# Three more score tiles on VectorE, a bank of its own for the first tile, and set-up work moved to GpSimd, in a softcap attention followed by a soft mixture of experts

## The chip, the cores and the metric

The kernel runs on one core of one Trainium2 chip. The metric is device time in microseconds (us). The engines in the profile are PE (TensorE's products, with PEld for its weight loads), DVE (VectorE), ACT (ScalarE), POOL (GpSimd) and SP (SyncE). Each engine works through its own instructions in the order written and waits at an instruction until what it needs from others is there.

## The reference

Attention over 8 batches, 12 heads, 448 positions and head dimension 64, with a soft cap of 30 on the scores, and then a soft mixture of 8 experts with 4 slots each:

```
scores = q @ k.T / 8;  scores = 30 * tanh(scores / 30)
attn = softmax(scores);  x = attn @ v            # laid out as 3584 x 768
logits = x @ phi                                  # 3584 x 32
slot_input = softmax(logits over tokens).T @ x    # 32 x 768
slot_out[e] = relu(slot_input[e] @ w1[e]) @ w2[e] # 768 -> 1024 -> 768
out = softmax(logits over slots) @ slot_out
```

Since the cap bounds the scores, the kernel takes exp without subtracting a maximum. The inputs are float32; the kernel works in bfloat16.

## The kernel before, in words

**Tiles.** Four heads form a quad; there are 24 quads, and each has two pairs of heads (`h` = 0 and 1), 48 pairs in all. A score tile is 128 key rows (64 of each of the pair's two heads) by 448 queries; a pair has seven of them. The 336 tiles go in the order `order` through 56 chunks of six tiles, and each chunk through two halves of three tiles. A half takes a score buffer of three banks of PSUM (`psS`, two buffers). One more bank (`psV`) is shared by the products with v, some transposes and filler products, and one (`psT`) by the other transposes.

**Stages of a chunk** (lines 831 to 861). ScalarE takes tanh of a half from PSUM into a buffer of SBUF (L326; five such buffers, one a chunk), and then exp in place for the tiles of a chunk that are its own (L330). Chunks 0 and 1 have their exp in their own round, later chunks one round later. PE makes the scores (L317) two halves ahead, and three rounds or so later the products of exp with v (`pv`, L581), whose right side is a block matrix `vbd` with v on its diagonal blocks, zeros elsewhere and a column of ones for the sums. VectorE divides by the sums (L588, L591). GpSimd casts v into the block matrix (L287), issues the loads of q and k (L184, as bfloat16) and of the experts' weights (L116, L120). SyncE's queue issues the loads of v (L194).

**Tiles on VectorE.** `SHARED` gives for some chunks the number of tiles, counted from the chunk's first, whose exp VectorE computes in place of ScalarE: a cubic in eight steps (`poly_exp`, L555 to L563), on one, two or three tiles at once. `POLY` writes out by hand at which place of which round each step stands; `(9, '>a'): ((9, 0), ...)` puts step 0 of chunk 9 behind what else stands at place `a` of round 9. The places of a round are, in order, 0, m, e (after the two tanh), a (after the first products with v), b (after the first half's scores), r, c, d (after the second half's scores); `<` and `>` put an item before or behind the others of its place.

**The order around it.** `at(j, place, function)` puts transposes, casts, loads and fillers at such places; `quad_in` does so for the casts, transposes and v casts of a quad. `transp` (L277, for the second quad L274) turns q and k on PE and copies the result out on VectorE (L279). A filler (`spare`, `busy`, `fill`: L814, L817, L611) is a product whose result nobody reads. `spare` takes a tile of `psV`.

**The start.** Quad 0 and quad 1 are loaded as float32 (`load_first`). Quad 0 is cast and turned in pieces by ScalarE, VectorE and PE (`first_half`, `first_pieces`, L231, L235, L237). Quad 1 is cast by VectorE (`cast`, L265), its v by GpSimd (L287, after which, for quad 0, SyncE loads the next v). The two block matrices are set by VectorE (`init_vbd`, L302 to L304) at place c of rounds 0 and 1. The first tanh is split: one tile, then two.

**After the attention** (from L862) come the last pairs, the slots' sums, the two layers of the experts and the output products.

Of the kernel before, what the change touches and what calls it, by code (L numbers as in the profile page):

```python
# [9 lines left out]
F32 = mybir.dt.float32  # L10
# [20 lines left out]
VW = 2 * W  # L31
# [6 lines left out]
def kernel(  # L38
# [20 lines left out]
    cap = float(cap)  # L59
    qk_scale = 1.0 / (DH ** 0.5)  # L60
# [178 lines left out]
    def first_half(h):  # L239
        for nm in ("k", "q"):  # L240
            if h == 0:
                qkT[nm, 0] = qk[0].tile([P, NT, P], BF16, name=nm + "T", tag=nm + "T")
        one = psT.tile([P, 8, P], BF16, name="ps1", tag="T")
        two = psV.tile([P, NT, P], BF16, name="ps2", tag="pv")
        if h == 0:

            three = boots[1][:, CS - 1, :].bitcast(BF16).rearrange("p (c q) -> p c q", q=P)
            first_pieces(h, (("cast", "q", 4, NT, act, None, 0), ("cast", "k", 0, CS, dve, None, 0),
                             ("cast", "q", 0, 4, dve, None, 0), ("turn", "q", 4, NT, pe, three, 0),
                             ("turn", "k", 0, CS, pe, two, 0), ("copy", "q", 4, NT, act, three, 0),  # L250
                             ("turn", "q", 0, 4, pe, one, 0), ("copy", "k", 0, CS, dve, two, 0),
                             ("cast", "k", CS, NT, act, None, 0), ("copy", "q", 0, 4, dve, one, 0),
                             ("junk", "k", 2, 0, pe, None, 0), ("turn", "k", CS, NT, pe, three, 3),
                             ("junk", "k", 1, 0, pe, None, 0), ("copy", "k", CS, NT, dve, three, 3)))
        else:
            first_pieces(h, (("cast", "k", 0, NT, dve, None, 0), ("cast", "q", 0, NT, dve, None, 0),
                             ("turn", "k", 0, NT, pe, two, 0), ("turn", "q", 0, NT, pe, one, 0),
                             ("copy", "k", 0, NT, dve, two, 0), ("copy", "q", 0, NT, dve, one, 0)))
            for nm in ("q", "k"):
                raws.pop((nm, 0)), casts.pop((nm, 0))  # L260
                load(nm, 2)

    def cast(nm):

        dve.tensor_copy(casts[nm, 1].rearrange("p c (h d) -> p h c d", h=2),  # L265
                        raws.pop((nm, 1)).rearrange("p h (c d) -> p h c d", d=DH))
# [32 lines left out]

    def init_vbd(n):  # L300
        t = vbds[n]
        dve.memset(t, 0.0)  # L302
        dve.memset(t[0:HP, :, :, DH:DH + 1], 1.0)
        dve.memset(t[HP:P, :, :, VW - 1:VW], 1.0)  # L304

    scores, exs, pvs, xq, xTs, lps = {}, {}, {}, {}, {}, {}

    def qk_chunk(i):
        sc = psS.tile([P, CS, 512], F32, name="sc", tag="sc")
        scores[i] = sc  # L310
        for u in range(CS):
            pr, c = order[i * CS + u]
            Q, h = divmod(pr, 2)
            r = slice(h * HP, h * HP + HP)
            for n in range(2):
                cs = slice(n * HP, n * HP + HP)
                pe.matmul(sc[cs, u, 0:S], qkT["k", Q][r, c, cs],  # L317
                          qkT["q", Q][r, :, cs], start=True, stop=True)

    def tanh_chunk(i):  # L320
        j, half = divmod(i, CH // CS)
        if half == 0:
            exs[j] = exps[j % NEX].tile([P, CH, S], BF16, name="ex", tag="ex")
        sc = scores.pop(i)
        for u0, u1 in ((0, 1), (1, CS)) if i == 0 else ((0, CS),):
            act.activation(exs[j][:, half * CS + u0:half * CS + u1, :].bitcast(F16),  # L326
                           sc[:, u0:u1, 0:S], ACT.Tanh, scale=qk_scale / cap)

    def exp_part(j, u0, u1):
        act.activation(exs[j][:, u0:u1, :], exs[j][:, u0:u1, :].bitcast(F16), ACT.Exp, scale=cap)  # L330
# [1 line left out]
    def exp_chunk(j):  # L332
# [1 line left out]

    SHARED = {3: (1, 0), 4: (3, 0), 6: (1, 0), 7: (3, 0), 9: (3, 0), 11: (2, 0), 12: (3, 0), 14: (3, 0),
# [4 lines left out]
    POLY = {(3, '>b'): ((3, 0), (3, 1)),  # L342
            (3, 'r'): ((3, 2),),
            (3, '<c'): ((3, 3),),
            (3, '>d'): ((3, 4),),
            (4, '>a'): ((3, 5), (3, 6), (4, 0)),
            (4, '>b'): ((3, 7),),
            (4, '<c'): ((4, 1),),
            (5, 'e'): ((4, 2), (4, 3)),
            (5, '>b'): ((4, 4),),  # L350
            (5, 'r'): ((4, 5),),
            (5, '>c'): ((4, 6),),
            (6, 'e'): ((6, 0), (6, 1)),
            (6, '>b'): ((6, 2), (6, 3)),
            (6, 'r'): ((4, 7),),
            (6, '>c'): ((6, 4), (6, 5)),
            (7, 'e'): ((7, 0), (6, 6), (6, 7)),
            (7, '>b'): ((7, 1),),
            (7, '>c'): ((7, 2), (7, 3)),
            (7, '>d'): ((7, 4),),  # L360
            (8, '>b'): ((7, 5),),
            (8, '>c'): ((7, 6),),
            (8, '>d'): ((7, 7),),
            (9, '>a'): ((9, 0),),
            (9, '>b'): ((9, 1),),
            (9, '>c'): ((9, 2),),
            (9, '>d'): ((9, 3),),
            (10, 'e'): ((9, 4),),
            (10, '>a'): ((9, 5),),
            (10, '>d'): ((9, 6),),  # L370
            (11, 'e'): ((11, 0), (9, 7)),
            (11, '>a'): ((11, 1), (11, 2)),
# [291 lines left out]
    es = {}  # L664
# [65 lines left out]
    def at(j, slot, f, *a):  # L730
        if j < 0:
            j, slot = 0, "b"
        aux.setdefault((j, slot), []).append((f, a))
# [16 lines left out]
                for n in range(2):  # L750
                    at(*v_in, vcast, Q, n)

    WHEN = {'k1': (-1, 'd'), 'q1': (0, 'b'), 'v1': (3, 'c'), 'k2': (2, 'b'), 'q2': (2, 'd'), 'v2': (7, 'b'), 'k3': (4, 'b'), 'q3': (5, 'b'), 'v3': (11, 'c'), 'x0': (5, 'a'), 'x1': (8, 'd'), 'x2': (10, 'a'), 'lg': (10, 'd'), 'ee': (11, 'm'), 'ss': (11, 'c'), 'et': (13, 'a'), 'en': (14, 'c'), 'es': (15, 'a')}

    for b in range(B):
        j, p = b * PER, 6 * b

        def when(nm):
            return j + WHEN[nm][0], WHEN[nm][1]

        if b == 0:
            quad_in(1, (0, "a"), (0, "b"), (0, "d"), (1, "a"), (2, "d"))
        else:
            quad_in(3 * b + 1, (j - 1, "b"), (j, "a"), when("k1"), when("q1"), when("v1"))
        quad_in(3 * b + 2, (j, "d"), (j + 1, "c"), when("k2"), when("q2"), when("v2"))
        quad_in(3 * b + 3, (j + 4, "a"), (j + 5, "a"), when("k3"), when("q3"), when("v3"))
        if b == 0:
            at(j + 1, "d", spare, 34)
            at(j + 2, "d", spare, 4)
        for k, slot, f, n in FILL:  # L770
            if (b or k > 2) and j + k < NCH - 1:
                at(j + k, slot, f, n)
        for hq in range(NQB if b < B - 1 else 1):
            at(*when(f"x{hq}"), x_transp, NQB * b + hq)
        if b == B - 1:
            at(j + 6, "a", x_transp, NQ - 2, (0,))
        if b < B - 1:
# [9 lines left out]
            at(j, slot, poly_exp, chunk, shared[chunk][0], n)  # L787
    for n, job in enumerate(wjobs):
        at(1 + n * (NCH - 5) // len(wjobs), "b", *job)
    for j, slot, n in ((0, "a", 10), (0, "c", 10), (1, "b", 10), (1, "c", 8)):  # L790
        at(j, slot, spare, n, 1)
    LATE = ((52, 'd', 3, 1), (54, 'd', 3, 3),)
    for j, slot, n, parts in LATE:
        at(j, slot, spare, n, parts)
    at(0, "c", init_vbd, 0)
    at(1, "c", init_vbd, 1)
    for n in range(2):
        at(0, "d", vcast, 0, n)
# [373 lines left out]
```

## Time and profile before

| what | value |
|---|---|
| time, median of three runs | 291.37 us (289.97 to 292.13) |
| time of the profiled execution | 290.2 us |
| its span | 288.4 us |
| busy: PE, DVE, ACT, POOL | 252.4, 239.7, 255.4, 134.6 us |
| first tanh starts | 7.00 us |
| mean granted clock of PE | 0.983 |

The span is what the profile covers of the execution's time; 1.8 us lie outside it. Busy times count each engine's own instructions, for PE with the fillers. The profile's views used below are the totals, the slices of the span, busy time per stretch, the instructions in order of time, and groups of instructions. In a row in order of time the first number is the start and the second the length; neighbours of the same kind may be merged into one row with a count, and a bracket at the end gives the idle time before it and what ended it.

### The profile page before, as it was taken

What the parts mean: (1) busy time and instruction counts of PE and PEld (TensorE: products, weight loads), DVE (VectorE), ACT (ScalarE), POOL (GpSimd) and SP (SyncE); (2) the same over time, 40 slices, a digit from 0 to 9 for tenths busy, and PEclk for the clock granted to TensorE, in tenths of its full rate; (3) what the DMA queues carried; (4) which work ended last, traced back from release to release, by engine and by line L of the source; (5) the groups of instructions that cost most, each with busy time, mean ns of one, the idle gap of its engine ahead of it and who ended that gap; (6) DMA issues with size and microseconds to landing.
All of it is one profiled execution on the core that took longest, in us unless ns stands there. A gap on an engine that the chain in (4) does not pass through costs nothing.

```text
span 288.4 us, 10848 instructions
## 1 busy us (share of the span) xinstructions
PE 252.4 (88%) x4753; PEld 171.2 (59%) x4753; DVE 239.7 (83%) x502; ACT 255.4 (89%) x211; POOL 134.6 (47%) x189
## 2 busy tenths in 40 slices
PE   8898789998999899989898999899899999998810
PEld 7555466656675667566656675666565767642400
DVE  3727899999999999999999999999999986347740
ACT  3999999999999999999999999999999997237720
POOL 4492655564755566555656646574563120200000
PEclk9999999999999999999999999999999999999985
DMA  7999999999999999999999999999999577989995
GB/s 215 263 190 204 195 204 228 226 198 199 232 229 197 200 231 222 224 199 230 226 217 201 223 226 207 215 221 220 212 174 224 114 246 250 406 316 384 414 424 240
DMA packets 58479, 68.11 MB, mean 236 GB/s; under 512 B 4161, under 2 KB 54593, under 8 KB 58433
## 3 DMA queue, kind: packets, MB, share of 16 engines
q0 software_dynamic: 42448, 35.31, 78.5%
q1 hardware_dynamic: 15696, 31.89, 32.0%
q8 instruction: 37, 0.61, 0.8%
q10 hardware_dynamic: 288, 0.23, 0.2%
q14 instruction: 10, 0.07, 0.1%
HBM read 91.72 MB, written 19.27 MB: 385 GB/s over the span
## 4 chain that ended last, share of the span: by engine, by line
DVE 30%; PE 27%; ACT 26%; issue 6%; DMA 3%; POOL 3%; DVEq 0%; ACTq 0%
ACT ex L326 15%; ACT ex L330 10%; PE pv L581 7%; DVE xq L591 5%; PE sc L317 4%; DVE xT L643 3%; DVE xp L561 3%; DVE ex L562 2%; DVE xp L559 2%; PE so_ps L1034 2%; DMA out_dram<-ob 2%; DVE qT L279 2%; PE hp L1006 2%; DVE ex L555 2%; DVE ex L563 2%
## 5 line engine op out<-in xcount | busy, mean ns | idle before, releaser
L326 ACT ACTIVATE ex<-sc 128x1344 f16<-128x1344 f32 (+1 forms) x113 | 150.1, 1459 | 2.0 <-PE sc L317 2.0
L330 ACT ACTIVATE ex<-ex 128x2688 bf16<-128x2688 f16 (+5 forms) x58 | 118.0, 2042 | 0.1
L581 PE MATMUL pv<-vbd,ex 128*128 128x130 bf16 (+1 forms) x1610 | 94.9, 211 | 11.1 <-POOL vbd L287 8.4
L581 PEld LDWEIGHTS <-ex 128*128 128x128 bf16 (+1 forms) x1680 | 75.8, 101 | 36.0 <-PE sc L317 9.0
L287 POOL CAST vbd<-vraw 64x896 bf16<-64x896 f32 x46 | 46.0, 1000 | 53.1 <-issue 23.2
L317 PE MATMUL sc<-qT,kT 64*64 64x448 bf16 x672 | 70.3, 359 | 0.6 <-ACT ex L326 0.4
L591 DVE TENSOR_TENSOR xq<-pv,rec 128x448 bf16<-128x448 f32 x46 | 28.7, 624 | 1.5
L317 PEld LDWEIGHTS <-kT 64*64 64x64 bf16 x672 | 23.8, 105 | 6.3 <-issue 4.3
L295 POOL MEMSET vbd<- 64x1 bf16 x22 | 4.0, 180 | 46.3 <-PE pv L581 46.3
L116 POOL DMA_DIRECT2D w1b<-in_moe_w_dram x32 | 25.0, 783 | 0.0
L559 DVE TENSOR_TENSOR xp<-xp,xf 128x1344 f16<-128x1344 f16 (+2 forms) x33 | 24.0, 726 | 0.6
L562 DVE TENSOR_TENSOR ex<-ex,xp 128x1344 uint16<-128x1344 uint16 (+2 forms) x33 | 24.0, 726 | 0.3
L561 DVE TENSOR_TENSOR xp<-xp,xf 128x1344 f16<-128x1344 f16 (+2 forms) x33 | 23.6, 716 | 0.7
L279 DVE COPY kT<-kps 128x896 bf16<-128x896 bf16 x23 | 14.2, 619 | 4.9 <-PE kps L277 4.6
L184 POOL DMA_DIRECT2D qb<-in_q_dram x22 | 16.6, 755 | 3.3 <-DMA kraw<-in_k_dram 3.3
L611 PE MATMUL pv<-ones 128*128 128x57 bf16 x390 | 16.4, 188 | 0.0
L563 DVE TENSOR_SCALAR ex<-ex 128x1344 uint16<-128x1344 uint16 (+2 forms) x33 | 16.2, 491 | 0.1
L184 POOL DMA_DIRECT2D kb<-in_k_dram x22 | 16.1, 734 | 0.2 <-issue 0.2
L277 PEld LDWEIGHTS <-qb 128*64 128x64 bf16 x308 | 10.1, 109 | 10.2 <-issue 10.2
L558 DVE TENSOR_SCALAR xp<-xf 128x1344 f16<-128x1344 uint16 (+2 forms) x33 | 15.8, 480 | 0.3
L555 DVE TENSOR_SCALAR ex<-ex 128x1344 uint16<-128x1344 f16 (+2 forms) x33 | 15.5, 470 | 0.7 <-ACT ex L326 0.6
L120 POOL DMA_DIRECT2D w2d<-in_moe_w_dram x21 | 15.8, 777 | 0.1
(126 smaller groups left out, 341.3 us busy)
## 6 DMA issues: line engine op xcount, KB each, us to landing
w1b<-in_moe_w_dram POOLq DMA_DIRECT2D x32, 384.0 KB, 8.7
vraw<-in_v_dram SPq DMA_DIRECT2D x44, 224.0 KB, 6.2
w2d<-in_moe_w_dram POOLq DMA_DIRECT2D x21, 384.0 KB, 8.6
w2t<-w2d SPq DMA_DIRECT2D x21, 384.0 KB, 7.4
out_dram<-ob SPq DMA_DIRECT2D x7, 768.0 KB, 7.8
qb<-in_q_dram POOLq DMA_DIRECT2D x22, 224.0 KB, 7.6
kb<-in_k_dram POOLq DMA_DIRECT2D x22, 224.0 KB, 6.5
w2b<-in_moe_w_dram POOLq DMA_DIRECT2D x11, 384.0 KB, 8.5
```

The costliest lines, as they stand in the source:

```text
L116: pool.dma_start(out=w1b[e][:, js, fs], in_=w1r[:, e, js, fs])
L184: pool.dma_start(out=t, in_=quad_ap(nm, Q))
L287: pool.tensor_copy(vbds[Q % 2][r, :, :, c0:c0 + DH], raw[r])
L317: pe.matmul(sc[cs, u, 0:S], qkT["k", Q][r, c, cs], qkT["q", Q][r, :, cs], start=True, stop=True)
L326: act.activation(exs[j][:, half * CS + u0:half * CS + u1, :].bitcast(F16), sc[:, u0:u1, 0:S], ACT.Tanh, scale=qk_scale / cap)
L330: act.activation(exs[j][:, u0:u1, :], exs[j][:, u0:u1, :].bitcast(F16), ACT.Exp, scale=cap)
L559: lambda: dve.tensor_tensor(p, p, f, op=ALU.mult),
L561: lambda: dve.tensor_tensor(p, p, f, op=ALU.mult),
L562: lambda: dve.tensor_tensor(y, y, p, op=ALU.add),
L563: lambda: dve.tensor_scalar(y, y, 128.0 / STEP, 128.0 * (127 - base), ALU.mult, ALU.add))
L581: pe.matmul(out_, exs[j][r, u, q0:q0 + (HP if tail else P)], v_, start=(c == 0 and g == gs[0] < NF), stop=(c == NT - 1), skip_group_check= ...
L591: dve.tensor_tensor(xq[Q][:, h, s0:s1, :], pv[:, 0:s1 - s0, 0:DH], rec.to_broadcast([P, s1 - s0, DH]), op=ALU.mult)
```

## The change

Five parts:

- `SHARED` gives VectorE two tiles of chunk 1 (none before) and two of chunk 3 (one before), 82 tiles in all instead of 79. `POLY` is written anew for chunks 1 to 12; from round 14 on it is the same.
- The first score tile of all is written to a tile of `psV`, a bank of its own, and the first tanh reads it there.
- The casts of the second quad's k and q go from VectorE to GpSimd, both now at place c of round 0, ahead of the first quad's v casts, which stand at the same place instead of d. Its transposes stand together at place d of round 0.
- Both block matrices are set by GpSimd, before the first products, the zeros through a float32 view.
- The counts of the fillers in rounds 0 to 2 are others, and one filler product ahead of the first scores is gone.

The entry `en` that leaves `WHEN` was not read.

```diff
-                             ("junk", "k", 1, 0, pe, None, 0), ("copy", "k", CS, NT, dve, three, 3)))
+                             ("copy", "k", CS, NT, dve, three, 3)))
...
-        dve.tensor_copy(casts[nm, 1].rearrange("p c (h d) -> p h c d", h=2),
-                        raws.pop((nm, 1)).rearrange("p h (c d) -> p h c d", d=DH))
+        pool.tensor_copy(casts[nm, 1].rearrange("p c (h d) -> p h c d", h=2),
+                         raws.pop((nm, 1)).rearrange("p h (c d) -> p h c d", d=DH))
...
-        dve.memset(t, 0.0)
-        dve.memset(t[0:HP, :, :, DH:DH + 1], 1.0)
-        dve.memset(t[HP:P, :, :, VW - 1:VW], 1.0)
+        pool.memset(t.rearrange("p h c w -> p (h c w)").bitcast(F32), 0.0)
+        pool.memset(t[0:HP, :, :, DH:DH + 1], 1.0)
+        pool.memset(t[HP:P, :, :, VW - 1:VW], 1.0)
...
+    own = {}
...
-        sc = psS.tile([P, CS, 512], F32, name="sc", tag="sc")
-        scores[i] = sc
+        scores[i] = psS.tile([P, CS, 512], F32, name="sc", tag="sc")
         for u in range(CS):
+            if i == u == 0:
+                own[0] = psV.tile([P, 1, 512], F32, name="sc0", tag="pv")
+            sc = own[0] if i == u == 0 else scores[i]
...
-                           sc[:, u0:u1, 0:S], ACT.Tanh, scale=qk_scale / cap)
+                           (own[0] if i == u0 == 0 else sc)[:, u0:u1, 0:S], ACT.Tanh,
+                           scale=qk_scale / cap)
...
-    SHARED = {3: (1, 0), 4: (3, 0), 6: (1, 0), ...
+    SHARED = {1: (2, 0), 3: (2, 0), 4: (3, 0), 6: (1, 0), ...
-    POLY = {(3, '>b'): ((3, 0), (3, 1)),
-            (3, 'r'): ((3, 2),),
-            (3, '<c'): ((3, 3),),
-            (3, '>d'): ((3, 4),),
-            (4, '>a'): ((3, 5), (3, 6), (4, 0)),
-            (4, '>b'): ((3, 7),),
...
+    POLY = {(1, 'e'): ((1, 0),),
+            (1, '>b'): ((1, 1), (1, 2)),
+            (1, 'r'): ((1, 3),),
+            (1, '<c'): ((1, 4),),
+            (1, '>c'): ((1, 5),),
+            (2, '>a'): ((1, 6),),
+            (2, '>c'): ((1, 7),),
+            (3, 'e'): ((3, 0), (3, 1), (3, 2)),
+            (3, '>b'): ((3, 3),),
+            (4, '>a'): ((3, 4), (3, 5), (3, 6), (4, 0)),
             (4, '<c'): ((4, 1),),
+            (5, 'e'): ((3, 7), (4, 2)),
+            (5, '>a'): ((4, 3),),
...
-            quad_in(1, (0, "a"), (0, "b"), (0, "d"), (1, "a"), (2, "d"))
+            quad_in(1, (0, "c"), (0, "c"), (0, "d"), (0, "d"), (2, "d"))
...
-            at(j + 1, "d", spare, 34)
-            at(j + 2, "d", spare, 4)
+            at(j + 1, "d", spare, 14)
+            at(j + 2, "d", spare, 5)
...
-    for j, slot, n in ((0, "a", 10), (0, "c", 10), (1, "b", 10), (1, "c", 8)):
+    for j, slot, n in ((0, "a", 5), (0, "c", 16), (1, "b", 12), (1, "c", 3)):
...
-    at(0, "c", init_vbd, 0)
-    at(1, "c", init_vbd, 1)
     for n in range(2):
-        at(0, "d", vcast, 0, n)
+        at(0, "c", vcast, 0, n)
...
     load_first()
+    for n in range(2):
+        init_vbd(n)
```

More of the change, by code (lines that the diff above doesn't have):

```diff
@@ L333, in exp_chunk @@
         exp_part(j, taken(j), CH)
-    SHARED = {3: (1, 0), 4: (3, 0), 6: (1, 0), 7: (3, 0), 9: (3, 0), 11: (2, 0), 12: (3, 0), 14: (3, 0),
[4 rows of a table removed]
-    POLY = {(3, '>b'): ((3, 0), (3, 1)),
-            (3, 'r'): ((3, 2),),
-            (3, '<c'): ((3, 3),),
-            (3, '>d'): ((3, 4),),
-            (4, '>a'): ((3, 5), (3, 6), (4, 0)),
-            (4, '>b'): ((3, 7),),
-            (4, '<c'): ((4, 1),),
[L349 to L354, printed above, removed]
+    SHARED = {1: (2, 0), 3: (2, 0), 4: (3, 0), 6: (1, 0), 7: (3, 0), 9: (3, 0), 11: (2, 0), 12: (3, 0),
[4 rows of a table added]
@@ new lines @@
+    POLY = {(1, 'e'): ((1, 0),),
[8 more added lines that the diff above has]
+            (4, '>a'): ((3, 4), (3, 5), (3, 6), (4, 0)),
+            (4, '<c'): ((4, 1),),
+            (5, 'e'): ((3, 7), (4, 2)),
+            (5, '>a'): ((4, 3),),
+            (6, 'e'): ((4, 4), (4, 5)),
+            (6, '>a'): ((6, 0), (4, 6), (6, 1)),
+            (6, '>b'): ((6, 2),),
@@ L355 @@
             (6, 'r'): ((4, 7),),
-            (6, '>c'): ((6, 4), (6, 5)),
-            (7, 'e'): ((7, 0), (6, 6), (6, 7)),
+            (6, '<c'): ((6, 3),),
+            (6, '>c'): ((6, 4),),
+            (6, '>d'): ((6, 5), (6, 6)),
+            (7, 'e'): ((7, 0), (6, 7)),
             (7, '>b'): ((7, 1),),
-            (7, '>c'): ((7, 2), (7, 3)),
-            (7, '>d'): ((7, 4),),
-            (8, '>b'): ((7, 5),),
+            (7, '>c'): ((7, 2),),
+            (7, '>d'): ((7, 3),),
+            (8, 'e'): ((7, 4),),
@@ L362 @@
+            (8, '>a'): ((7, 5),),
             (8, '>c'): ((7, 6),),
-            (8, '>d'): ((7, 7),),
-            (9, '>a'): ((9, 0),),
+            (9, '>a'): ((9, 0), (7, 7)),
             (9, '>b'): ((9, 1),),
[L366 to L372, printed above, removed]
+            (9, '<c'): ((9, 2),),
@@ L373 @@
+            (10, 'e'): ((9, 3),),
+            (10, '>a'): ((9, 4),),
+            (10, '>b'): ((9, 5),),
+            (10, '>c'): ((9, 6),),
+            (11, 'e'): ((11, 0), (9, 7), (11, 1)),
+            (11, '>a'): ((11, 2),),
             (11, '<c'): ((11, 3),),
-            (11, '>d'): ((11, 4), (11, 5)),
-            (12, 'e'): ((11, 6),),
+            (11, '>d'): ((11, 4), (11, 5), (11, 6)),
             (12, '>a'): ((11, 7), (12, 0)),
@@ L378 @@
             (12, '<c'): ((12, 2),),
-            (13, 'e'): ((12, 3),),
-            (13, '>b'): ((12, 4), (12, 5)),
+            (12, '>c'): ((12, 3),),
+            (13, '>b'): ((12, 4),),
+            (13, '>c'): ((12, 5),),
             (13, '>d'): ((12, 6),),
@@ L751, in quad_in @@
                     at(*v_in, vcast, Q, n)
-    WHEN = {'k1': (-1, 'd'), 'q1': (0, 'b'), 'v1': (3, 'c'), 'k2': (2, 'b'), 'q2': (2, 'd'), 'v2': (7, 'b'), 'k3': (4, 'b'), 'q3': (5, 'b'), 'v3': (11, 'c'), 'x0': (5, 'a'), 'x1': (8, 'd'), 'x2': (10, 'a'), 'lg': (10, 'd'), 'ee': (11, 'm'), 'ss': (11, 'c'), 'et': (13, 'a'), 'en': (14, 'c'), 'es': (15, 'a')}
+    WHEN = {'k1': (-1, 'd'), 'q1': (0, 'b'), 'v1': (3, 'c'), 'k2': (2, 'b'), 'q2': (2, 'd'), 'v2': (7, 'b'), 'k3': (4, 'b'), 'q3': (5, 'b'), 'v3': (11, 'c'), 'x0': (5, 'a'), 'x1': (8, 'd'), 'x2': (10, 'a'), 'lg': (10, 'd'), 'ee': (11, 'm'), 'ss': (11, 'c'), 'et': (13, 'a'), 'es': (15, 'a')}
     for b in range(B):
```

8 rows, old and new, of the table SHARED are left out of this document.

## The prediction

> **What bounds the kernel now.** I read the page's totals and slices first, for who is busy when.
>
> ```profile
> span 288.4 us, 10848 instructions
> PE 252.4 (88%) x4753; PEld 171.2 (59%) x4753; DVE 239.7 (83%) x502; ACT 255.4 (89%) x211; POOL 134.6 (47%) x189
> ...
> DVE  3727899999999999999999999999999986347740
> ACT  3999999999999999999999999999999997237720
> ```
>
> A slice is 7.2 us. ScalarE is full from the second slice to the 33rd; VectorE has room only in slices 2 to 5, and is then just as full. PE at 88% has its fill-in products in that number. So the attention part has two co-bounds, and an edit that shifts work from one to the other pays only where the receiver is idle. The second view, busy time per stretch, says where (the columns are the stretch, its length, then busy time and instruction count of PE, PEld, DVE, ACT, POOL):
>
> ```profile
> 12.00:16.90 4.90, 4.43 (x50) 2.86 (x49) 2.25 (x8) 4.87 (x5) 4.77 (x6) 1.00 1.10 157
> 16.90:21.40 4.50, 4.23 (x60) 2.61 (x59) 1.50 (x4) 4.50 (x4) 4.39 (x7) 1.00 1.19 216
> 21.40:26.00 4.60, 4.00 (x83) 2.60 (x82) 2.87 (x9) 4.60 (x4) 0.55 (x1) 1.00 1.24 204
> 26.00:31.00 5.00, 3.87 (x88) 2.84 (x83) 4.12 (x8) 5.00 (x5) 2.37 (x3) 1.00 1.25 204
> 31.00:36.30 5.30, 4.02 (x63) 2.04 (x58) 4.93 (x11) 5.30 (x4) 4.32 (x6) 1.00 1.08 184
> 36.30:44.40 8.10, 7.30 (x156) 5.33 (x154) 7.69 (x18) 8.10 (x8) 4.82 (x8) 1.00 1.19 216
> ```
>
> VectorE idles 2.65, 3.00, 1.73 and 0.88 us in the first four stretches and 0.37 in the fifth; ScalarE idles in none. The third view, VectorE in order of time (start, length, then in brackets the idle time before it and what ended it), names the waits:
>
> ```profile
> 19.20 0.62 DVE L279 COPY kT<-kps 128x896 bf16<-128x896 bf16 x1 [4.28 <-PE kps L277]
> 20.49 0.62 DVE L279 COPY qT<-qps 128x896 bf16<-128x896 bf16 x1 [0.67 <-PE qps L277]
> ...
> 23.20 0.20 DVE L588 RECIPROCAL rec<-pv 128x7 f32<-128x7 f32 x1 [1.58 <-PE pv L581]
> ...
> 26.33 0.62 DVE L279 COPY kT<-kps 128x896 bf16<-128x896 bf16 x1 [0.37 <-PE kps L277]
> ...
> 31.27 0.62 DVE L279 COPY qT<-qps 128x896 bf16<-128x896 bf16 x1 [0.67 <-PE qps L277]
> 53.86 0.72 DVE L555 TENSOR_SCALAR ex<-ex 128x896 uint16<-128x896 f16 x1 [0.22 <-ACT ex L326]
> ```
>
> Between 31.27 and 53.86 VectorE waits nowhere above 0.2 us, and then 0.22 us for a tanh. So at 53.64 it has just caught up with ScalarE. From there the two programs are unchanged: **whatever both engines have gained at 53.6 us, the end gains**, and the smaller gain counts.
>
> **ScalarE, term by term.** The first tanh:
>
> ```profile
> 6.61 0.82 PE L317 MATMUL sc<-qT,kT 64*64 64x448 bf16 x6
> ...
> 7.00 0.54 ACT L326 ACTIVATE ex<-sc 128x448 f16<-128x448 f32 x1 [1.49 <-PE sc L317]
> ```
>
> The earliest of the merged products, at 6.61, writes the third tile of the first half; by the 0.38 us of the pair quoted next it ends at 6.99, and the tanh of only the first tile starts at 7.00. It waited for all three tiles of the buffer. The first pair starts earlier:
>
> ```profile
> 6.20 0.38 PE L317 MATMUL sc<-qT,kT 64*64 64x448 bf16 x2
> ```
>
> It ends at 6.58, so with a bank of its own the first tanh can start about 6.6: **0.4 us**. The next tanh needs the products that end at 6.99, and the first takes until about 7.0: nothing is lost behind it. The removed filler ahead of the products may give 0.1 more; bounds 0 to 0.5, I take 0.4.
>
> The three tiles fewer of exp, start to start (the next instruction's start tells the real cost, as ScalarE's records overlap):
>
> ```profile
> 9.57 2.44 ACT L330 ACTIVATE ex<-ex 128x2688 bf16<-128x2688 f16 x1
> 11.92 2.45 ACT L326 ACTIVATE ex<-sc 128x1344 f16<-128x1344 f32 x2
> ...
> 26.11 2.11 ACT L330 ACTIVATE ex<-ex 128x2240 bf16<-128x2240 f16 x1
> 28.07 2.51 ACT L326 ACTIVATE ex<-sc 128x1344 f16<-128x1344 f32 x2
> ```
>
> Six tiles cost 2.35, five 1.96, so a tile is 0.37 to 0.39. Chunk 1 loses two (0.75), chunk 3 one (0.37): 1.12. ScalarE gains **1.5 us** by chunk 4, if it is fed.
>
> **VectorE, term by term.** It loses two casts of the second quad and two block memsets with their ones, and gains the eight steps of two tiles in chunk 1 and a second tile in chunk 3:
>
> ```profile
> L302 DVE MEMSET vbd<- 128x910 uint32 x2 | 1.6, 817 | 0.3
> ...
> L265 DVE CAST casts<-raw 128x896 bf16<-128x896 f32 x2 | 1.2, 624 | 0.0
> ```
> ```profile
> L559 DVE TENSOR_TENSOR xp<-xp,xf 128x896 f16<-128x896 f16 x10 | 6.6, 665 | 0.1
> ...
> L560 DVE TENSOR_SCALAR xp<-xp 128x896 f16<-128x896 f16 x10 | 3.8, 383 | 0.0
> ...
> L561 DVE TENSOR_TENSOR xp<-xp,xf 128x448 f16<-128x448 f16 x5 | 2.0, 404 | 0.1
> ...
> L558 DVE TENSOR_SCALAR xp<-xf 128x448 f16<-128x448 uint16 x5 | 1.3, 267 | 0.1
> ```
>
> Of each size there are eight such groups, costliest and cheapest shown; their means add to 3.96 us for two tiles and 2.55 for one. The records overlap a little, so 3.7 to 4.0 for chunk 1 and 1.0 to 1.4 more for chunk 3; I take 3.8 and 1.2. The 3.1 us removed earn nothing: the 4.28 us wait follows them. The added 3.8 must fit before that wait's end, and after the copies of the second quad's transposes, for which PE's order sets the time:
>
> ```profile
> 9.23 0.62 DVE L237 COPY qT<-ps 64x896 bf16<-64x896 bf16 x1
> 9.37 0.72 PE L817 MATMUL junk<-ones 128*128 128x128 bf16 x10 [0.33 <-DVE kT L237]
> ...
> 10.02 0.57 PE L317 MATMUL sc<-qT,kT 64*64 64x448 bf16 x6
> ...
> 11.87 0.56 PE L274 MATMUL kps<-ident,casts 128*128 128x128 bf16 x7
> ```
>
> The q copy ends at 9.85, three score tiles take 0.57 to about 10.5, then 16 fillers of 0.07 to 11.65, three more tiles to 12.2; k's transposes run to 12.75, q's to 13.3, q's copy ends at about 14.0. Steps 0 to 6 of chunk 1 (3.4) then run to 17.4. The wait's end itself moves: it hangs on the tanh of chunk 2's first half (ScalarE frees the buffer, PE makes scores and turns k), which gains 0.4 + 0.75 = 1.15, so the 19.20 copy comes at 18.05. **The cover is 0.6 us wide**; beyond it, each us passes on.
>
> From 18.05 to the catch-up: before, 19.20 to 53.64 is 34.44 us, 3.29 of it the waits of 0.67, 1.58, 0.37 and 0.67. The work is therefore 31.15, plus 1.2 and the last step of chunk 1 (0.4): 32.75. Waits that remain, walking through the new order: 0.3 at the q copy, 0.45 at the reciprocal (three steps of chunk 3 now stand before it, and the PE products it needs come 1.15 earlier), 0.2 and 0.25 around the next k copy, 0.5 behind xT: 1.7. That is 18.05 + 32.75 + 1.7 = 52.5, a gain of 1.15; VectorE had 0.22 in hand there, so the end may gain 1.15 + 0.22 = **1.4**, just under ScalarE's 1.5. Bounds: with all 3.3 us of waits kept it is 54.1, 0.2 later than 53.86; with none, ScalarE's 1.5 rules.
>
> **GpSimd, PE and the queues.** Cost of the moved work:
>
> ```profile
> 12.07 1.94 POOL L287 CAST vbd<-vraw 64x896 bf16<-64x896 f32 x2 [3.75 <-DVE vbd L302]
> ...
> 32.41 1.61 POOL L287 CAST vbd<-vraw 64x896 bf16<-64x896 f32 x1
> ...
> L989 POOL MEMSET hpad<- 128x2048 bf16 x1 | 1.8, 1809 | 10.2 <-PE slpl L710 10.2
> ```
> ```profile
> 5.05 0.83 POOL L184 DMA_DIRECT2D qb<-in_q_dram  x1 [3.29 <-DMA kraw<-in_k_dram]
> ...
> 7.62 0.70 POOL L184 DMA_DIRECT2D kb<-in_k_dram  x1 [0.19 <-issue]
> ```
>
> The memsets (910 elements, by the 0.88 ns per element of L989 0.8 us each, at twice that by bytes 1.6) fit in GpSimd's 3.29 us wait, which ends at 5.05: free, at worst 0.4 late for loads that have many us in hand. A cast of 64 partitions takes 0.97, once 1.61; 128 partitions aren't shown. Bounds: 0.97 (GpSimd's time goes by elements per partition) to 3.2 (twice the slowest row); I take 1.0, the nearest row. The sources land late:
>
> ```profile
> raw<-in_k_dram SPq DMA_DIRECT2D x1, 448.0 KB, 6.0
> raw<-in_q_dram SPq DMA_DIRECT2D x1, 448.0 KB, 6.7
> ```
>
> Issued at 2.11 and 2.59, they land at 8.1 and 9.3, so the casts end at 9.1 and 10.3, before PE asks at 12.2. Behind them on GpSimd stand the two v casts and then the load of k for quad 3, which slips from 7.62 to about 13 us; what it brings is first copied, transposed, at 26.33, twice the landing times above later. The weight loads come behind it and start about when they did (14 us). The fillers in the loop's first three chunks fall from 76 products' worth to 55, 1.5 us of PE at 0.07; PE's gaps there shrink by ScalarE's 1.15, and I price the difference at 0.1 to either side.
>
> [...]
>
> **The rivals.** (1) VectorE becomes the bound: the waits of the third view don't shrink, because PE, not VectorE, sets them. By the bound above it reaches the catch-up at 54.1, 0.2 late: 291.6 us. For it: the waits all name PE. Against: the PE work they name starts from a tanh that is earlier. (2) Slower: the casts at 128 partitions cost 3.2 us. The q cast then ends at 8.1 + 6.4 = 14.5, its transposes and copy at 15.8, and chunk 1's steps push the k copy from 18.05 to 19.2; 19.2 + 32.75 + 1.7 to 3.3 is 53.65 to 55.25, which is 0.2 early to 1.4 late, and as the waits would then stay I take 1.3 late: 292.7. It decides once the q cast ends after 13.3, above 2.6 us a cast. For it: 1.61 was seen with half the partitions; against: 12.07 to 14.01 held two such casts. (3) The own bank does nothing, the tanh still waiting for six products: gain 1.0, 290.4.
>
> **How the numbers follow.** The profiled execution took 290.2 us with its span of 288.4; less 1.4 that is 288.8. The median of the three runs shown is 291.37, 1.2 above it, and the same gain from there is **290.0**, my number. Chances: forecast 0.55, rival 1 0.2, rival 2 0.15, rival 3 0.1. The three runs lie 1.4 below to 0.8 above their median. The forecast's own range is 0.9 to 1.7 us of gain (the copies' waits larger by 0.5, or the fillers and the removed product adding 0.2), 289.7 to 290.5; with the runs' spread added below (less 1.4, and 0.4 for waits that I don't see going) and rival 2 above, it is 287.9 to 292.8. About 1% (2.9 us) is what a measurement of this kernel tells from no change. Faster by more than that needs the forecast and a low draw: 0.13. Slower by more needs rival 2 and a high draw or an unseen stall: 0.09. The rest, 0.78, is within.
>
> **What would show it.** First tanh at 6.6; exp of chunk 1 at 1792 elements, 1.6 us; no VectorE wait of 4 us near 19; casts on GpSimd of about 1 us ending before 10.5; the k copy near 18.0; the tanh wait of VectorE at about 52.4 instead of 53.86. Wrong it would be if VectorE shows no wait for tanh any more and ScalarE shows waits for scores, or if PE waits for the casts.

## The result, and the profile after

The changed kernel takes 288.40 us (median of nine, 287.76 to 289.59), the kernel before, run beside it, 289.97 (median of nine). The ratio of the times is 0.9938, with a 95% interval of 0.9913 to 0.9963: faster by 0.6%, 1.6 us by the medians. The profiled execution took 287.77 us with a span of 286.0, against 290.2 and 288.4.

Totals and slices of the changed kernel, as shown above of the one before:

```profile
span 286.0 us, 10843 instructions
PE 250.6 (88%) x4745; PEld 170.3 (60%) x4745; DVE 242.9 (85%) x502; ACT 254.1 (89%) x211; POOL 139.1 (49%) x197
...
DVE  3498999999999999999999999999999986346740
ACT  4999999999999999999999999999999997237720
```

VectorE's empty third slice (a 2 before) is a 9 now: the hole is filled. Busy time per stretch says the same; DVE is the third pair of numbers behind the stretch's length:

```profile
12.00:16.90 4.90, 4.48 (x53) 2.71 (x50) 4.29 (x9) 4.87 (x5) 4.85 (x7) 1.00 1.08 172
16.90:21.40 4.50, 4.15 (x76) 2.72 (x71) 4.26 (x8) 4.50 (x4) 4.44 (x6) 1.00 1.21 193
21.40:26.00 4.60, 4.01 (x85) 2.70 (x82) 4.00 (x9) 4.60 (x4) 0.40 (x2) 1.00 1.24 206
```

2.25, 1.50 and 2.87 us busy have become 4.29, 4.26 and 4.00; ScalarE stays full. The start, ScalarE and then VectorE in order of time:

```profile
6.33 0.54 ACT L329 ACTIVATE ex<-sc 128x448 f16<-128x448 f32 x1 [0.81 <-PE sc L320]
```
```profile
12.40 0.62 DVE L279 COPY kT<-kps 128x896 bf16<-128x896 bf16 x1 [2.84 <-PE kps L274]
...
16.76 1.23 DVE L571 TENSOR_TENSOR ex<-ex,xp 128x896 uint16<-128x896 uint16 x1
17.92 0.61 DVE L279 COPY kT<-kps 128x896 bf16<-128x896 bf16 x1
...
25.08 0.62 DVE L279 COPY kT<-kps 128x896 bf16<-128x896 bf16 x1 [0.21 <-PE kps L277]
25.94 0.21 DVE L597 RECIPROCAL rec<-pv 128x7 f32<-128x7 f32 x1 [0.23 <-PE pv L590]
...
28.51 0.62 DVE L652 COPY xT<-xps 128x896 bf16<-128x896 bf16 x1 [0.29 <-PE xps L643]
...
30.65 0.20 DVE L597 RECIPROCAL rec<-pv 128x7 f32<-128x7 f32 x1 [0.21 <-PE pv L590]
...
52.37 0.39 DVE L564 TENSOR_SCALAR ex<-ex 128x896 uint16<-128x896 f16 x1
```

The 4.28 us wait is gone. The step that waited for a tanh at 53.86 stands at 52.37 and waits for none: VectorE no longer catches up with ScalarE there. Its only such wait behind it ends at 138.80, the last of three before at 140.61. ScalarE itself waits for nothing that the profile names from the first tanh to 241 us.

**Where the time went.** I use one mark through all runs, ScalarE's first exp of the logits in round 11, and its seventh, in round 53:

```profile
53.56 0.43 ACT L668 ACTIVATE E<-lps 128x128 bf16<-128x128 f32 x1
...
207.71 1.29 ACT L326 ACTIVATE ex<-sc 128x1344 f16<-128x1344 f32 x1 [0.49 <-PE sc L317]
...
228.49 0.35 ACT L668 ACTIVATE E<-lps 128x128 bf16<-128x128 f32 x1
```
```profile
51.87 0.35 ACT L677 ACTIVATE E<-lps 128x128 bf16<-128x128 f32 x1
...
226.09 0.35 ACT L677 ACTIVATE E<-lps 128x128 bf16<-128x128 f32 x1
```

The first view is of before, the second of the changed kernel. At round 11 the gain is 1.69 us: 0.67 at the first tanh, 1.02 behind it. At round 53 it is 2.40; the 0.71 more are not the change's: this one execution of before covers round 11 to 53 in 174.93 us, the changed kernel in 174.22, and the twelve kernels below in 174.07 to 174.46, among them the one that differs from before only by the new bank (174.07). Of the 0.71, 0.49 are the wait for scores at 207.71. So about 1.7 of before's 2.4 us longer span are the change, near the 1.6 of the medians.

### The profile page after: what moved, and what is told of

It is laid out like the page before. It is cut to its first block, busy times and chain, and to the rows that moved or that the text cites. A ratio compares the mean times of both kernels' runs of the same rounds, so it can differ in the third digit from the quotient of the medians.

```text
span 286.0 us, 10843 instructions
## 1 busy us (share of the span) xinstructions
PE 250.6 (88%) x4745; PEld 170.3 (60%) x4745; DVE 242.9 (85%) x502; ACT 254.1 (89%) x211; POOL 139.1 (49%) x197
## 4 chain that ended last, share of the span: by engine, by line
DVE 29%; PE 27%; ACT 26%; issue 7%; POOL 3%; DMA 3%; DVEq 0%; ACTq 0%
ACT ex L329 14%; ACT ex L334 11%; PE pv L590 7%; DVE xq L600 5%; PE sc L320 4%; DVE ex L571 3%; DVE xp L570 3%; DVE xT L652 3%; DVE xp L568 2%; DMA out_dram<-ob 2%; PE so_ps L1043 2%; DVE ex L564 2%; PE hp L1015 2%; DVE qT L279 2%; POOL vbd L287 2%
## 5 line engine op out<-in xcount | busy, mean ns | idle before, releaser
L329 ACT ACTIVATE ex<-sc 128x1344 f16<-128x1344 f32 (+1 forms) x113 | 148.0, 1424 | 0.8 <-PE sc L320 0.8
L334 ACT ACTIVATE ex<-ex 128x2688 bf16<-128x2688 f16 (+5 forms) x58 | 114.9, 1989 | 0.1
L320 PE MATMUL sc<-qT,kT 64*64 64x448 bf16 x672 | 71.3, 359 | 0.5 <-DVE qT L279 0.4
L571 DVE TENSOR_TENSOR ex<-ex,xp 128x1344 uint16<-128x1344 uint16 (+2 forms) x34 | 25.2, 741 | 0.4
L568 DVE TENSOR_TENSOR xp<-xp,xf 128x1344 f16<-128x1344 f16 (+2 forms) x34 | 25.0, 735 | 0.6
L570 DVE TENSOR_TENSOR xp<-xp,xf 128x1344 f16<-128x1344 f16 (+2 forms) x34 | 24.5, 720 | 0.8
L572 DVE TENSOR_SCALAR ex<-ex 128x1344 uint16<-128x1344 uint16 (+2 forms) x34 | 17.3, 508 | 0.1
L567 DVE TENSOR_SCALAR xp<-xf 128x1344 f16<-128x1344 uint16 (+2 forms) x34 | 17.0, 500 | 0.4
L120 POOL DMA_DIRECT2D w2d<-in_moe_w_dram x21 | 15.8, 780 | 0.4 <-issue 0.4
```

Of the source, the lines that this page charges most:

```text
L320: pe.matmul(sc[cs, u, 0:S], qkT["k", Q][r, c, cs], qkT["q", Q][r, :, cs], start=True, stop=True)
L568: lambda: dve.tensor_tensor(p, p, f, op=ALU.mult),
L570: lambda: dve.tensor_tensor(p, p, f, op=ALU.mult),
L571: lambda: dve.tensor_tensor(y, y, p, op=ALU.add),
```

## The experiments

All compute the whole reference. "Mark" is the exp of round 11; "Less the first tanh" takes out that the start itself comes earlier or later from run to run: with the same code up to it, the first tanh came between 6.13 and 6.74. Each mark is of one profiled execution. Four kernels with the changed kernel's tiles lie within 0.12 us of each other in the mark less the first tanh (45.42 to 45.54), three with the tiles of before within 0.05 (46.54 to 46.59). I read the single parts from it, since the ratios' intervals, 0.5 to 1.0 us to either side, are wider than most of them.

| kernel | first tanh | mark | mark less first tanh | span | ratio to before |
|---|---|---|---|---|---|
| before | 7.00 | 53.56 | 46.56 | 288.4 | 1 |
| changed | 6.33 | 51.87 | 45.54 | 286.0 | 0.9938 (0.9913 to 0.9963) |
| only own bank | 6.62 | 53.21 | 46.59 | 287.7 | 0.9983 (0.9965 to 1.0002) |
| shared bank | 6.49 | 51.91 | 45.42 | 286.9 | 0.9927 (0.9896 to 0.9958) |
| 79 tiles | 6.13 | 52.67 | 46.54 | 287.1 | 0.9954 (0.9923 to 0.9985) |
| casts on VectorE | 6.50 | 51.95 | 45.45 | 286.5 | 0.9937 (0.9905 to 0.997) |
| casts, memsets on VectorE | 6.39 | 53.32 | 46.93 | 287.7 | 1.0002 (0.9974 to 1.0031) |
| old fillers | 6.37 | 52.71 | 46.34 | 287.3 | 0.9948 (0.9915 to 0.9981) |
| no fillers | 6.33 | 53.15 | 46.82 | 288.4 | 1.0005 (0.9977 to 1.0033) |
| v casts later | 6.74 | 52.16 | 45.42 | 287.0 | 0.995 (0.993 to 0.997) |
| casts three times | 6.23 | 57.00 | 50.77 | 292.2 | 0.9992 (0.996 to 1.0024) |
| only 82 tiles | 6.96 | 57.22 | 50.26 | 292.0 | 1.0096 (1.0062 to 1.013) |
| 83 tiles | 6.21 | 57.05 | 50.84 | 291.4 | 1.0089 (1.0054 to 1.0123) |
| 83 tiles, turned earlier | 6.33 | 53.21 | 46.88 | 287.4 | 0.9934 (0.991 to 0.9959) |

### The bank of its own

Shared bank again, in the changed kernel:

```diff
-            if i == u == 0:
-                own[0] = psV.tile([P, 1, 512], F32, name="sc0", tag="pv")
-            sc = own[0] if i == u == 0 else scores[i]
+            sc = scores[i]
```

> The changed kernel, with the first score tile back in the buffer of its half. My theory: the tanh of one tile waits for all six products again, so it starts about 0.4 us after the 6.33 of the changed kernel, at 6.7; ScalarE stays that much late, VectorE too from the first tanh it needs, and the span is 286.4 instead of 286.0. Rival (the early start came from the removed filler alone): first tanh still near 6.3, span unchanged.

And the own bank alone, in the kernel before (the same lines the other way):

> The kernel before, with the bank of its own for the first score tile and nothing else. My theory: first tanh at 6.6 instead of 7.00, and since VectorE's chain hangs on the tanh of chunk 2 both engines gain it: span 288.0 instead of 288.4. Rival (VectorE bound): it had 0.2 in hand at the catch-up, so ScalarE's gain is lost behind 0.2 and VectorE's tanh wait of 53.86 is gone. Rival (the bank does nothing): first tanh at 7.00.

The first products of the two and of the changed kernel, one row each, and then the first tanh of the two, with the shared bank first:

```profile
5.69 0.76 PE L318 MATMUL sc<-qT,kT 64*64 64x448 bf16 x6
```
```profile
6.20 0.38 PE L320 MATMUL sc<-qT,kT 64*64 64x448 bf16 x2
```
```profile
5.91 0.57 PE L320 MATMUL sc<-qT,kT 64*64 64x448 bf16 x4
```
```profile
6.49 2.53 ACT L327 ACTIVATE ex<-sc 128x448 f16<-128x448 f32 x3 [1.19 <-PE sc L318]
```
```profile
6.62 2.54 ACT L329 ACTIVATE ex<-sc 128x448 f16<-128x448 f32 x3 [1.11 <-PE sc L320]
```

With the shared bank the products start at 5.69 and the tanh at 6.49, 0.80 later, as before (6.20 and 7.00). With the own bank it is 0.42 in both kernels that have it (6.20 and 6.62, 5.91 and 6.33). So the bank is worth **0.38 us** at the first tanh. The other 0.29 of the changed kernel's 0.67 are 0.16 for the removed filler (from the last transposes ahead of the products to the products it is 0.50 us before, 5.70 to 6.20, and 0.34 in the changed kernel, 5.57 to 5.91) and 0.13 by which those transposes start earlier. In the kernel before, the bank's 0.38 arrive at the mark as 0.35 (53.56 to 53.21): theory held, VectorE did not swallow it (the ratio alone, 0.9983, isn't clear of 1). In the changed kernel the expected loss did not show: the mark moved by 0.04, but this run's products also started 0.22 earlier than the changed kernel's, so the bank's worth there isn't measured.

### The tiles

```diff
-    SHARED = {1: (2, 0), 3: (2, 0), ...
+    SHARED = {3: (1, 0), ...              # and POLY of before
```

> The changed kernel, with the tile counts and the step places of before (79 tiles). My theory (ScalarE and VectorE bound together, ScalarE fed): the first tanh stays at 6.33, ScalarE is 0.75 late from round 2 and 1.1 late from round 4 on, and the span is about 287.1. Rival (VectorE alone is the bound): VectorE has 5 us less to do, so the span stays at 286.0 or falls.

The mark less the first tanh is 46.54, that of before, 1.00 above the changed kernel's. The three tiles are worth 1.0 of the 1.12 that they take from ScalarE; the rest the changed kernel loses at one place (from its tanh of round 6, at 29.83, to the exp behind it, at 32.28, are 2.45 us instead of 2.34; the profile names no wait there). VectorE alone as the bound is refuted: with 6 us less to do on it (busy 236.9 instead of 242.9) the kernel gains nothing. By the ratios alone, 0.9954 and 0.9938, the two can't be told apart.

The tiles alone in the kernel before, with casts and memsets on VectorE and the fillers of before:

> The kernel before, with 82 tiles and the new step places and nothing else; casts and memsets stay on VectorE, the fillers stay many. My theory: ScalarE saves 1.1 us, but the 34 filler units hold the scores of round 3, and the memset stands between the steps of chunk 1, so VectorE's k copy comes at about 18.9 to 19.3 (19.20 before) and the rest of VectorE's extra 1.2 us is paid by its waits: span 287.6 to 288.6. Rival (the parts are independent): ScalarE's 1.1 us come out in full, span 287.3.

The span is 292.0, some 4 us above what I expected and 3.6 above before, and the mark is 3.7 late. In its trace a VectorE step takes 1.04 us instead of 0.38, at 13.18, where GpSimd is busy (in the kernel before with the v casts, 12.07 to 14.01); the q copy follows at 14.14, PE waits 1.04 us for it, and the granted clock falls from 1.00 to 0.50. The next kernel shows the same chain most plainly.

### One tile more, and PE's clock

```diff
-    SHARED = {1: (2, 0), ...
-    POLY = {(1, 'e'): ((1, 0),),
+    SHARED = {0: (1, 0), 1: (2, 0), ...
+    POLY = {(0, 'e'): tuple((0, n) for n in range(8)),
+            (1, 'e'): ((1, 0),),
```

> The changed kernel, with one more tile on VectorE: the first of chunk 0, all eight steps at place e of round 0 (83 tiles). VectorE waits 2.84 us before 12.40, and eight steps of one tile take about 2.6. My theory: ScalarE gains another 0.37 from the exp of chunk 0 on; VectorE is busy without a wait at 17.92 in the changed kernel, but that copy waits for a tanh chain that is 0.37 earlier only where VectorE can follow; I expect 0.1 to 0.4 gained: span 285.6 to 285.9. Rival (VectorE is the bound from 12 us on): span 286.0 or a little more.

It is slower than before. Busy time per us of this kernel (PE first; the granted clock is the number behind POOL's count, 1.00 when full):

```profile
12.00:13.00 1.00, 1.00 (x16) 0.60 (x13) 0.90 (x4) 1.00 (x2) 1.00 (x2) 1.00 1.69 194
13.00:14.00 1.00, 0.13 (x2) 0.00 (x0) 0.93 (x3) 0.97 (x2) 1.00 (x3) 1.00 0.95 156
14.00:15.00 1.00, 0.00 (x0) 0.12 (x1) 1.00 (x2) 0.93 (x1) 1.00 (x2) 0.78 1.07 190
15.00:16.00 1.00, 0.84 (x6) 0.46 (x6) 0.96 (x3) 0.23 (x1) 0.95 (x2) 0.50 1.15 265
...
23.00:24.00 1.00, 1.00 (x16) 0.72 (x14) 0.27 (x1) 0.77 (x1) 1.00 (x2) 0.50 1.24 206
24.00:25.00 1.00, 0.94 (x9) 0.50 (x8) 0.89 (x2) 1.00 (x2) 0.94 (x2) 0.60 1.17 175
```

PE stands from 13.13 to 15.15, waiting for the q copy. **The clock falls to 0.50 within that wait and stays there until 24.8** (the means of 0.78 and 0.60 in their us put the two changes at 14.56 and 24.8); ScalarE, fed by PE, is busy 0.23 us of one in which it was full. In the kernel with the tiles alone the clock was at 0.50 from 15.8 to 22.6; it fell when PE, from 14.80, was at work again. With the late copies this puts the mark 5.2 us behind the changed kernel's here; how the two share that isn't shown. It stayed down for 10.2 us here and 6.8 us there. PE had been idle for only 1.4 us when it fell here, and yet a stand of 1.84 us did not bring it down, as the last experiment shows.

Why did PE wait? In the same kernel, GpSimd and VectorE in order of time:

```profile
9.47 0.28 DVE L565 TENSOR_SCALAR ex<-ex 128x448 uint16<-128x448 f16 x1
9.71 1.94 POOL L287 CAST vbd<-vraw 64x896 bf16<-64x896 f32 x2 [0.20 <-DMA vraw<-in_v_dram]
9.79 0.99 DVE L567 TENSOR_SCALAR xf<-ex 128x448 uint16<-128x448 uint16 x1
...
10.81 0.98 DVE L568 TENSOR_SCALAR xp<-xf 128x448 f16<-128x448 uint16 x1
```

Two steps of 0.27 us took 0.99 and 0.98, each ending about 0.1 behind a v cast of 0.97. The 1.43 us that they took too long are most of the 1.55 by which the q copy is late (14.49, 12.94 in the changed kernel). My theory took the eight steps at 2.6 us and had no term for this. What of VectorE's 2.84 us of waiting lies beside GpSimd's v casts, in the changed kernel from 10.55 on, was no free room for these two steps. In the changed kernel the addition at 16.76 takes 1.23 instead of 0.62, beside v casts of 1.16 and 1.24.

### The fillers

```diff
-            at(j + 1, "d", spare, 14)
-            at(j + 2, "d", spare, 5)
+            at(j + 1, "d", spare, 34)
+            at(j + 2, "d", spare, 4)
...
-    for j, slot, n in ((0, "a", 5), (0, "c", 16), (1, "b", 12), (1, "c", 3)):
+    for j, slot, n in ((0, "a", 10), (0, "c", 10), (1, "b", 10), (1, "c", 8)):
```

> The changed kernel, with the filler counts of before in rounds 0 to 2 (the filler removed ahead of the first scores stays removed). My theory: the 34 units at place d of round 1 now hold PE 1.1 us too long, the scores for round 3 come at about 17.8 instead of 16.66, ScalarE waits about 0.6 us for them near 17.7 and VectorE's k copy slips by 1.1: span 286.5 to 287.1. Rival (fillers only fill gaps): span 286.0.

The mark is 0.84 late, 0.80 less the first tanh. VectorE waits at the k copy again, PE being late:

```profile
18.81 0.62 DVE L279 COPY kT<-kps 128x896 bf16<-128x896 bf16 x1 [0.58 <-PE kps L277]
```

Without any in rounds 0 to 2 (the six calls of `spare` for these rounds taken out):

> The changed kernel, with no filler products at all in rounds 0 to 2. Theory from the three runs whose granted clock fell to 0.50 after PE had idled for 1.5 to 2 us near 13 us: PE stands idle more here, the clock falls to 0.50 between 11 and 16 us and stays there for 7 to 10 us, and the span is 290 to 293. Rival (fillers only fill gaps, as I priced them at 0.1): clock 1.00 and span 286.0.

```profile
14.00:15.00 1.00, 0.50 (x6) 0.07 (x2) 0.97 (x2) 1.00 (x1) 1.00 (x3) 0.99 0.93 158
15.00:16.00 1.00, 0.00 (x0) 0.00 (x0) 0.93 (x3) 1.00 (x2) 1.00 (x2) 0.50 1.09 196
...
21.00:22.00 1.00, 1.00 (x20) 0.75 (x18) 0.93 (x3) 1.00 (x1) 0.48 (x1) 0.60 1.26 204
```

The clock fell at 15.0, as expected, and came back at 21.8; the mark lost 1.28 and the whole gain of the change is gone (ratio 1.0005). Too many fillers cost 0.8 us, none 1.3.

### The set-up work on GpSimd

Casts and memsets back on VectorE, at the places of before but for the casts, which stay at place c:

```diff
-        pool.tensor_copy(casts[nm, 1]...
+        dve.tensor_copy(casts[nm, 1]...
...
-        pool.memset(t.rearrange(...).bitcast(F32), 0.0)      # and the ones
+        dve.memset(t, 0.0)
...
+    at(0, "c", init_vbd, 0)
+    at(1, "c", init_vbd, 1)
```

> The changed kernel, with the second quad's casts and the block memsets back on VectorE (casts and first memset at place c of round 0, second memset at place c of round 1). My theory: casts and first memset, 2.1 us, fit the 2.84 us in which VectorE waits before 12.40; the second memset, 1.0 us, stands between the steps of chunk 1 and makes the k copy of 17.92 up to 1 us late, of which later waits of 0.2 to 0.3 us each (0.9 in all) take back most: span 286.0 to 286.9. Rival (the move to GpSimd pays for itself): all 3.1 us come back, span 288 or more.

Then the casts alone:

> The changed kernel, with only the second quad's two casts back on VectorE; the memsets stay on GpSimd. Theory: they lie in the 2.84 us in which VectorE waits before 12.40, so nothing is lost: k copy at 17.9, ScalarE's tanh of round 11 at 50.7, span 286.0; the 1.45 us that ScalarE lost at round 11 with both parts back came from the second memset. Rival (the casts cost on VectorE): tanh of round 11 at 51.5 or later.

With both back, VectorE shows the second memset between the steps, and the k copy at 19.37, 1.45 after the changed kernel's:

```profile
16.39 0.82 DVE L302 MEMSET vbd<- 128x910 uint32 x1
...
18.22 1.23 DVE L571 TENSOR_TENSOR ex<-ex,xp 128x896 uint16<-128x896 uint16 x1
19.37 0.61 DVE L279 COPY kT<-kps 128x896 bf16<-128x896 bf16 x1
```

From 16.39 to 17.56 the memset and its ones take 1.17 of the 1.45; the rest is the later start and steps that took longer. The mark is 1.45 late too: **what VectorE loses at 17.9 passes on in full**, my 0.9 us of later waits that would take it back did nothing. The way is through PE, which now waits 1.58 us for the k copy instead of 0.18, and on to ScalarE, which waits for scores 0.22 us before 30.46 and here:

```profile
32.55 1.29 ACT L329 ACTIVATE ex<-sc 128x1344 f16<-128x1344 f32 x1 [0.79 <-PE sc L320]
```

With only the casts back nothing is lost (45.45 against 45.54): they lie in the wait before the k copy at 12.57, which is 1.65 instead of 2.84, while GpSimd, without them, is idle. The casts' move was not needed, the second memset's was the part that paid.

Two more on GpSimd. The casts done three times over:

```diff
-        pool.tensor_copy(casts[nm, 1]..., raws.pop((nm, 1))...)
+        raw = raws.pop((nm, 1))
+        for _ in range(3):
+            pool.tensor_copy(casts[nm, 1]..., raw...)
```

> The changed kernel, with each of the two moved casts done three times on GpSimd (about 3.0 us a cast; the result is the same). My second rival priced such casts: from 2.6 us a cast on they would cost, up to 1.3 us late against before. With what the changed trace shows (no cover left at the k copy of 17.92) my theory is now: the q cast ends at about 14, its copy at 15.2 instead of 13.55, the steps of chunk 1 and the k copy follow 1.6 us late, waits of 0.9 us further on take a part back: span 286.7 to 287.6. If GpSimd's time for the casts never mattered: 286.0.

The q copy slipped to 14.37 and the next k copy to 22.24. This kernel's executions fall into two groups, six of ten at 289.4 to 290.5 us with a mean granted clock of 0.981 to 0.986, and four at 292.2 to 294.8 with 0.964 to 0.973. The profile is of the second group, with the clock at 0.50 from 14.6 to 24.8; the ratio is of the first and the fastest of the second. By its median, 289.70 against 290.21 of the kernel before beside it (0.9982), the first group loses 1.3 us on the changed kernel (0.9982 less 0.9938, of 290), within the 0.7 to 1.6 that I expected. The v casts of the second quad, put at place c of round 3:

> The changed kernel, with the second quad's two v casts at place c of round 3 instead of d of round 2. In the changed kernel the addition on two tiles beside them took 1.23 us at 16.76 (0.62 elsewhere), and the casts 1.23 each (0.97 elsewhere). Theory (the two engines hold each other up): the addition takes 0.62, VectorE's k copy comes about 0.2 to 0.3 earlier than 17.92, then bound by PE, and the span gains 0.1 to 0.3 at most. Rival (the longer time was something else): the addition still takes 1.2, nothing moves.

```profile
16.86 2.22 POOL L287 CAST vbd<-raw 64x896 bf16<-64x896 f32 x2
```
```profile
16.96 1.30 DVE L571 TENSOR_TENSOR ex<-ex,xp 128x896 uint16<-128x896 uint16 x1
```

GpSimd runs ahead of the rounds, so the casts started about where they had, at 16.86 (16.36 in the changed kernel, whose first tanh is 0.41 earlier), and the addition beside them took 1.30. The edit didn't part the two. The kernel with the old fillers does, since its casts run earlier:

```profile
15.11 1.99 POOL L287 CAST vbd<-raw 64x896 bf16<-64x896 f32 x2
```
```profile
15.28 1.00 DVE L569 TENSOR_SCALAR xp<-xp 128x896 f16<-128x896 f16 x1
16.32 1.25 DVE L570 TENSOR_TENSOR xp<-xp,xf 128x896 f16<-128x896 f16 x1
17.61 0.62 DVE L571 TENSOR_TENSOR ex<-ex,xp 128x896 uint16<-128x896 uint16 x1
```

Here the addition, behind the casts, takes 0.62 again, and the two steps beside them take 1.00 and 1.25 instead of 0.39 and 0.63. So the longer time goes with the casts and not with the step, and casts that come earlier only bring it to other steps.

### A version that might beat both

```diff
-            quad_in(1, (0, "c"), (0, "c"), (0, "d"), (0, "d"), (2, "d"))
+            quad_in(1, (0, "c"), (0, "c"), (0, "c"), (0, "c"), (3, "c"))
...
-    SHARED = {1: (2, 0), ...
+    SHARED = {1: (3, 0), ...
...
-    for j, slot, n in ((0, "a", 5), (0, "c", 16), (1, "b", 12), (1, "c", 3)):
+    for j, slot, n in ((0, "a", 5), (0, "b", 8), (0, "d", 12), (1, "b", 12), (1, "c", 3)):
```

> A version that may beat both: the changed kernel with the second quad's transposes at place c of round 0, ahead of the second half's scores instead of behind them, 8 fillers at place b and 12 at d in the place of the 16 at c, the second quad's v casts at place c of round 3, and three tiles of chunk 1 on VectorE (83 in all). Theory: the q copy ends near 12 instead of 13.5, the steps start when the tanh they need is done (12.5), so three tiles end before the k copy of 17.7; ScalarE gains 0.37 more: tanh of round 11 at 50.2 to 50.5, span 285.4 to 285.8. Rival (VectorE is the bound behind 18 us whatever comes before): tanh of round 11 at 50.7 or later, no gain. If PE is left idle too long near 13 us, the clock halves and the span is above 290.

```profile
11.92 0.61 DVE L279 COPY qT<-qps 128x896 bf16<-128x896 bf16 x1
...
16.05 2.58 POOL L287 CAST vbd<-raw 64x896 bf16<-64x896 f32 x2
...
16.35 1.46 DVE L570 TENSOR_TENSOR xp<-xp,xf 128x1344 f16<-128x1344 f16 x1
...
17.84 1.49 DVE L571 TENSOR_TENSOR ex<-ex,xp 128x1344 uint16<-128x1344 uint16 x1
...
19.26 0.61 DVE L279 COPY kT<-kps 128x896 bf16<-128x896 bf16 x1
```

The copies came as early as meant, but two steps beside the v casts took 1.46 and 1.49 instead of 0.86, and the k copy is 1.34 late, as is the mark. The profile is of the slowest of four executions (289.23 us; the others 287.7 to 288.4), and by the ratio this version can't be told from the changed kernel. PE stood still for 1.84 us from 18.1 here, and the clock stayed at 1.00.

## Why the prediction was right, point by point

The changed kernel takes 288.40 us, inside the stated range. The number was 290.0, and the 1.6 between them are no flaw of the gain: 1.4 of them are the median of before, 291.37 over three runs and 289.97 over nine. For that reason the time lies below the forecast's own 289.7 to 290.5 and inside only by what was added for the runs' spread. The gain of 1.4 us behind the number stands against 1.6 by the medians and 1.69 at the mark, and as forecast it is under 1%. The step at the catch-up was foretold at 52.4 and stands at 52.37. Some of that is luck: terms were off both ways.

- **First tanh**, 0.4 foretold, 0.67 measured. The bank's part was right to 0.02 (0.38). The filler that I priced at up to 0.1 brought 0.16, and 0.13 came from the transposes' earlier start, which is chance.
- **ScalarE's three tiles**, 1.12: 1.00 arrive at the mark. Right.
- **"The smaller gain counts"**: VectorE, put at 1.4, is 1.49 early at the step of the catch-up and ScalarE, put at 1.5, 1.69 at the mark. VectorE's gain didn't hold the end back: at 138.80 it has caught up again.
- **"The cover is 0.6 us wide"** was wrong. The steps end at 17.99, at the k copy, not at 17.4, since the addition took 1.23 beside a v cast. No cover was left, and with the second memset back on VectorE the k copy came 1.45 later. That I let the removed 3.1 us "earn nothing" is right for the casts (nothing lost with them back) and wrong for the second memset.
- **Waits that remain**, 1.7: they are 0.21, 0.23, 0.29 and 0.21, 0.94 in all. The work between the k copy and the catch-up was 33.5 us (52.37 less 17.92 less 0.94), 0.75 above my 32.75. The two errors cancel, which is luck. Most of the second is the second tile of chunk 3, put at 1.2: from each step's start to the next instruction's, its eight steps take 4.35 us instead of 2.51, 1.84 more.
- **The casts at 128 partitions**: 0.93 us each, about as for 64 (0.97, half of two in a row); the memsets 0.86 each, near the 0.8 by elements. Both lower bounds held.

```profile
L265 POOL CAST casts<-raw x2: 929/930/932, 7.9 to 9.0; 128x896 bf16<-128x896 f32 x2
```

- **Fillers at 0.1 to either side** is the step that failed: the old counts cost 0.8, none at all 1.3, and PE's clock, which I nowhere priced, costs up to 5.2 us together with the late copies that go with its fall from 1.00 to 0.50.
- **Rival 1** (VectorE the bound, no gain) fell as put, though the 1.45 us by which the second memset made the k copy late passed on in full. **Rival 2** was not met, its casts being 0.93; at three times that they bring the time back to about that of before (0.9992), less than the 1.3 us above it that I priced, and in the slower execution that was profiled the mechanism was another than mine, the clock at 0.50 for 10.2 us. **Rival 3** fell.
- **The sign of being wrong** came half: at 52.37 VectorE shows no wait for a tanh any more, but ScalarE shows no wait for scores.

## What to carry to other kernels

Where two engines are full, an empty stretch of one may be less room for the other's work than it looks: here VectorE steps of 0.27 us took 0.98 to 0.99 beside GpSimd's v casts, so look at what GpSimd does in that stretch before filling it. Try the count of products without use in both directions: in this kernel the counts of before held up the products behind them and cost 0.8 us, and without any PE's granted clock was at 0.50 for 6.8 us and the cost was 1.3. Read the granted clock as well as the wait when an edit makes PE wait longer: with 83 tiles it went from 1.00 to 0.50 within a wait of 2.02 us.

## What the runs showed of the hardware that was not expected

The granted clock went from 1.00 to 0.50 at 14.56 with 83 tiles, after PE had stood idle for 1.4 us; at 15.8 with the tiles alone, 1.0 us behind the end of a stand of 1.04 us; at 15.0 without fillers, PE having been busy 0.39 to 0.64 of each us from 11.00 and having stood from 14.5. It came back after 10.2 us in the first and 6.8 us in the other two. Yet a stand of 1.84 us at 18.1 left it at 1.00 in the version turned earlier, and with the casts three times over it seems to have fallen in four of ten executions, of which one was profiled. Six of 60 further executions of the kernel before have a mean granted clock of 0.970 to 0.974 and took 291.9 to 293.6 us, so it may fall there too; none of them was profiled. What decides it beside the length of the stand is open. A GpSimd cast of 896 elements a partition took 0.93 us on 128 partitions; on 64, two in a row took 1.94, 0.97 each. Two VectorE steps of 0.27 us beside such a pair took 0.99 and 0.98 with 83 tiles.
